# Linear attention and a token/channel mixer: releasing three weight loads by another landing, and moving one eviction in VectorE's order

## The chip, the core and the metric

The kernel runs on one core of one Trainium2 chip. The metric is the time of one execution on the device, in microseconds (us); the medians below are over runs of the same kernel.

The engines are called as the profile calls them: PE (TensorE: matmul), PEld (its weight loads), DVE (VectorE), ACT (ScalarE), POOL (GpSimd), SP (SyncE). SP and POOL issue most of the DMA transfers here: those of SP are in the profile's queue q1, those of POOL in q0.

## The reference

There are 8 batch elements ("images"), 8 heads, 576 positions and a head dimension of 64, all float32. Linear attention comes first, then a mixer over tokens and over channels:

```python
phi = lambda x: np.where(x > 0, x, np.exp(x) - 1.0) + 1.0        # elu + 1
q_p, k_p = phi(q), phi(k)
kv  = einsum('bhsd,bhse->bhde', k_p, v);  z = k_p.sum(axis=2)
x   = einsum('bhsd,bhde->bhse', q_p, kv) / (einsum('bhsd,bhd->bhs', q_p, z)[..., None] + 1e-6)
x   = x.transpose(0, 2, 1, 3).reshape(8, 576, 512)
u   = x + (relu(x.transpose(0, 2, 1) @ w_tok1) @ w_tok2).transpose(0, 2, 1)   # 576 -> 256 -> 576
out = u + relu(u @ w_ch1) @ w_ch2                                            # 512 -> 1536 -> 512
```

## The kernel before

The eight images are worked on one after another, but overlapped: while PE does the channel products of image n, the other engines load and prepare image n+1. Nothing is reordered by a scheduler. Every step has a short name (a token) in a table, and a long string, `ORDER`, lists the tokens; the kernel calls them in that order (`for name in ORDER.split(): tok[name]()`). Each engine runs its own instructions in the order in which this list issues them, and waits on semaphores where data or buffers are not ready. An instruction that waits holds up all that stands behind it on the same engine.

The tokens that matter here, the first digit being the image:

- `1Lk0 1Lk1 1Lv1 1Lq0 1Lq1 1Lv0` (line 228): SP's loads of image 1, in this order; each brings one half (piece 0 or 1, four heads, 576 KB) of k, v or q into `k_raw`, `v_raw`, `q_raw`. The first waits for a piece of the first channel weight. `2Lq0` is the first load of image 2; it waits for piece 1 of the second channel weight `wc2` (the table `GATE`).
- `1qx0`, `1qa0`, `1qb0` (lines 252, 256, 262): elu + 1 of q's piece 0 in three steps. `x` is the exponential on ACT into `e`; `a` is max(q + 1, 1) on DVE into `y`; `b` is their minimum on DVE into `qp`. There is one `y` buffer only. `1qx1 1qa1 1qb1` are the same for piece 1, `1k..` for k.
- `1v0`, `1v1` (line 275): v's pieces to bfloat16, `1v0` on DVE and `1v1` on ACT.
- `1Q00 1Q01`, then `1Q10 1Q11` (line 320): transposes of `qp` on PE, nine for each piece; `1Qc0.` and `1Qc1.` (line 326) copy them out of PSUM, on ACT for piece 0 and on DVE for piece 1. `1K` (line 302): k times v on PE; it reads both pieces of `kp` and of the converted v.
- `0ma.`, `0mb.` (line 686): the first channel product of image 0, twelve column blocks with two matmuls each in the `a` and the `b` half. `0r.` (lines 693 and 695): relu and eviction of a block from PSUM into `cr`, on DVE for blocks 3, 6 and 9, on ACT for the others.
- `0q0` to `0q11` (line 747): the second channel product of image 0, by blocks of its contraction. `0q0` does four matmuls: row blocks 0 and 1 with contraction blocks 0 and 1. Row block 1 is summed in PSUM bank 0, which block 9 of the first product has filled, so the second matmul of `0q0` waits until `0r9` has emptied it.
- `B0 B1 B2` (line 1126): POOL's loads of pieces 1, 2 and 3 of `wc2` (`load_wc2`). Piece i holds contraction blocks 3i to 3i + 2, and is converted to bfloat16 on the way, 384 KB as written. Piece 0 is issued early. Of the other three, only `B0` has a gate, but all are in POOL's one queue:

```python
WGATE = {1: ('in', 'q', 1, 0)}
...
live["wc2", i] = after(nc.gpsimd.dma_start(out=wc2[:, m * i:m * (i + 1), :], in_=...),
                       live[WGATE[i]] if i in WGATE else None)
```

`after` makes the DMA wait for the landing of the named transfer: here of q's piece 0 of image 1. Behind `B2` on POOL come `ws02 ws04 ws14 ...` (line 816), differences of `wc2` blocks that later products use.

Around the change the list reads `... G23 0mb9 0r5 0ma11 0mb11 1qa0 1qx0 B0 0r9 0q0 B1 0r11 1qb0 B2 1qx1 1qa1 1Q00 1Q01 0q1 1Qc01 1v0 1Qc00 0q2 1qb1 1v1 1Q10 1Q11 1K ...`.

Of the kernel before, what the change touches and what calls it, by code (L numbers as in the profile page):

```python
# [30 lines left out]

GATE = {'1k0': ('wc1', 0), '2q0': ('wc2', 1), '4q0': ('u', 2, 1), '7q0': ('u', 5, 1)}

WGATE = {1: ('in', 'q', 1, 0)}

ON_DVE = {'1v0', '2v1', '0r3', '0r6', '0r9', '1r5', '1r8'}

# [28 lines left out]
ORDER = """A2 A0 A1 A3 A4 A5 A6 A8 A9 A7 A10 A12 A13 A14 A11 A16 A17 A15 A19 A18 A21 A20 A22 A23 A24 A25 A26 A27 A28 A29  # L66
A30 A33 A31 A32 A35 A34 A36 A37 A38 1Lk0 A39 1Lk1 1Lv1 A40 1Lq0 A41 1Lq1 A42 1Lv0 A43 0ma0 At2 0ma1 At3 0ma3
0mb1 0mb0 0ma6 0r0 0mb3 0r1 1ka0 0ma7 1kx0 0ma2 0ma8 0mb6 1kb0 0mb2 0r3 0mb8 0mb7 0r6 0r8 0ma4 0r7 G21 0gt
1kx1 G22 0ma9 0gv 0ma10 0mb4 1ka1 0r2 0ma5 0r4 G11 0mb10 1kb1 0mb5 0r10 G23 0mb9 0r5 0ma11 0mb11 1qa0 1qx0 B0
0r9 0q0 B1 0r11 1qb0 B2 1qx1 1qa1 1Q00 1Q01 0q1 1Qc01 1v0 1Qc00 0q2 1qb1 1v1 1Q10 1Q11 1K 1Qc11 2Lq0 ws02  # L70
1Qc10 0q3 2Lq1 1Kc0 1Kc1 2Lv0 ws04 1n20 1n01 2Lk0 1nc20 0q4 2Lk1 1nc01 2Lv1 1n10 0q5 1nc10 1n00 0q6 1nc00 1n11
0q7 1nc11 2qx0 1n21 ws14 0q8 1nc21 1f0 2qx1 2qa0 1f1 wt2 3Lq0 G24 0q9 1fr1 2qb0 1fr0 0q10 2qa1 2v0 G12 1h01
2qb1 1h00 1hu01 2qT1 ws00 0q11 1hu00 0z1 2kx0 1h10 2qT0 ws10 0z0 1h11 1hu10 1t0 1hu11 1t1 3Lv0 ws24 1g2 1tc1
1tc0 1t2 3Lq1 1t3 1gu2 1ma9 1tc3 ws12 0z2 1ma1 1ma5 1tc2 1ma4 0z3 1mb1 2v1 0o1 1mb5 1r1 1ma7 2ka0 2kx1 1mb7
G01 3Lk0 1ma10 0o0 G03 3qx0 1mb4 2kb0 0ut 1ma2 2ka1 1r4 1mb10 wt0 3Lk1 1mb2 1r7 1ma3 3Lv1 1r2 2kb1 1mb9 1r10
1ma8 3qa0 0uc 1mb8 1r5 ws20 1r9 2K 1r8 1mb3 2Kc0 2Kc1 3qb0 1ma6 1r3 2n ws30 2nd 1mb6 T00 2o0 ws34 1r6 2n1
1ma11 Tr00 2o1 ws22 1mb11 2ne 3v0 2n0 1ma0 1mb0 3qa1 T01 4Lv0 1r0 2n2 ws32 1r11 1p10 3qx1 2f0 1w13 G02 Tr01
4Lq1 1w10 1p11 3kx1 3qb1 1p20 3ka0 3kx0 2f1 1w20 G14 2fr0 4Lk0 T02 1w23 3qT1 1w30 1p50 Tr02 3kb0 1p51 2fr1
3qT0 1c0 1w40 1p21 4qx1 2g1 3ka1 1c2 1eZ 1p60 3v1 G13 1p61 2gu1 2g0 1c1 3kb1 2uT1 1p31 2gu0 4kx0 1p30 3K 4qa1
2uT0 1p71 3Kc1 1eY 3Kc0 4v0 1p70 4qb1 4Lv1 4Lq0 3n 1hY 1eW 4Lk1 U00 3ne 5Lv0 3nd 1hZ U01 3n2 U02 3o0 1hW 3n1  # L80
1p40 3n0 2x01 2x11 2s1 3o1 1p41 V0 2y11 2x02 2y01 2s2 1eX 2x15 2x21 2s3 1o 2x12 2y21 2x16 2y12 2x06 2y16 2s4
2x05 2y06 2y02 2x17 2y15 4qa0 2x26 4qx0 2x25 2y17 2x07 G04 3f0 2y25 4qb0 2y05 4ka0 2y26 4qT1 2x14 2x03 2y07
2y14 2x13 3fr0 4qT0 3f1 2y13 4kb0 2x27 5Lq0 3fr1 2y03 2x23 5Lk0 2x04 2y27 2x22 2y04 4ka1 2x24 4kx1 2y22 3gt
3g1 2y23 2y24 2w10 2p20 2w12 2p10 2w20 3gu1 2p50 2p11 2w22 3uT1 2p51 3gt1 2c0 3g0 4v1 4kb1 2w30 2p60 2p61 3gu0
2p21 2c1 3gt0 3uT0 4K 2eZ 2p70 4Kc1 2c2 2w40 3ut 2p71 4Kc0 4n 2eW 5Lq1 2p30 4nd 2hW 5Lk1 4ne 2p31 5Lv1 4n0
2p41 2hZ 4o0 4n1 2p40 3x11 3s1 3x21 4o1 3y11 3s2 3x01 4n2 5kx0 3x16 3x12 2eY 3y21 T12 3s3 5v0 2eX 2hY 3x15
3y12 3x05 3y16 3x02 5ka0 2o 3y01 3x26 3y02 6Lk0 3x25 3x06 5kb0 3y25 W0 3x22 3y26 5ka1 3x23 3y06 3x17 3y22 3y15
3x27 3s4 3y05 3x07 3y17 5kx1 T11 3y27 3x03 3y07 Tr12 6Lk1 3x14 Tr11 3y03 3x24 5kb1 3x13 3y24 4f0 3y13 5qx0
5qa0 4f1 3y14 3y23 4fr0 5qb0 3x04 4fr1 T10 3w12 3y04 5qa1 4g0 Tr10 3w10 5v1 4g1 4gu0 5qx1 3p20 4gu1 4uT0 5K
6kx1 3p21 3w20 4uT1 5qb1 3p10 5Kc1 6kx0 3w22 3p11 5qT1 3eZ 3p50 3c0 6ka1 3p51 5Kc0 5qT0 3w40 U10 3c2 3w30 U11  # L90
6Lq0 6Lq1 6kb1 U12 4s1 6ka0 3p31 V1 3p30 7Lk0 4s2 6Lv1 3p61 3eY 6Lv0 3p60 6kb0 7Lk1 5n 3c1 5nd 3hY 3p71 5ne
3p70 5n0 3hZ 4x02 5o0 3eW 4x01 4x21 5n2 4y01 3hW 3p40 4y21 4y02 4x06 6qx0 5n1 4x05 4x26 4y06 6qa1 3p41 4y05
5o1 4x11 4s3 4x03 3eX 4y11 4x25 4y26 4s4 3o 4x07 4y03 6qx1 4x12 4y07 4x16 4x27 4y25 4y12 4x04 4y16 6qb1 5f0
4y04 6qa0 6v0 4x15 4y27 4x23 4w10 4y15 4x17 6qb0 5fr0 4x22 4y17 4x13 6qT0 4x24 4y23 4x14 4y24 4y13 6qT1 5f1
4y14 4y22 6v1 7ka1 4p20 4w12 4p21 5fr1 4w20 5g1 4w22 4p10 5gu1 4p11 5g0 4w40 5uT1 4c0 4eZ 5gt 6K 5gu0 4hZ 4p50
6Kc1 6Kc0 5gt1 5uT0 7kx1 4p51 5gt0 4p60 4c2 4w30 7Lv0 6n 7kx0 7Lq0 7kb1 4p61 7Lq1 6ne 7Lv1 4p30 6nd 4c1 6n2
4p31 4p71 6n0 4p70 4eY 5x11 6o1 5x02 6o0 5y11 5s1 5x12 4eW 5x01 5s2 5x15 5y01 4hW 6n1 4p40 7v0 5x16 5y12 4p41
5y16 7ka0 5x06 5y15 5s3 5x21 5y02 7F12 5x13 5y21 4eX 4hY 5x17 5y06 5x05 5y17 5x26 5y05 7kb0 4o 5x07 5y26 5x25
5y13 5x03 5y25 5s4 5x27 7qa0 7qx0 6f0 5y07 7v1 7qb0 5x14 6f1 7qa1 7qx1 5y27 5x04 6fr0 5y03 5x22 6fr1 5x23 7qb1
5y14 5x24 5y22 5y04 7qT1 7K 5y23 5p10 7Kc1 7Kc0 5w10 7qT0 5y24 6g0 5w30 6g1 5w12 5w20 5p20 6gu1 5p50 5p11 5w22  # L100
6uT1 6gu0 5p21 5c0 5p51 5eZ 6uT0 5p60 5c2 5w40 7n 5hZ 7nd 5p61 7ne 5p31 7n1 5c1 7F15 5p30 7o1 7o0 5p70 7n2
5p71 6s1 5eY 6x21 6x01 6s2 5hY 7n0 6x11 6y01 6x12 6y11 6x06 6y21 6s3 6x15 5eW 6y06 6x16 6x02 5hW 6y16 6x05
6y02 5p40 6y12 7F14 6x26 6s4 6y15 6x17 7F11 6x25 6y26 6x07 7F10 6y05 5p41 6y25 W1 6x13 5eX 6x03 6y07 6x23 7F13
6x27 6y03 6x22 5o 6x04 6y22 7f0 6y17 6y23 7f1 7fr0 6y27 6y04 6x14 6y13 7fr1 6x24 6y14 6w30 7g0 6y24 6w10 6p10
7gu0 7g1 6w12 7uT0 6p11 6w20 6p50 6w22 6c0 5ut 6p20 7gu1 6p51 7F2 7uT1 7gt 6p61 7gt0 6p60 6w40 7x12 6c1 7gt1
6p21 6c2 7F4 7ut 6p71 6eZ 7x11 6p70 7s1 6hZ 7x02 6eW 7x01 6p30 7y01 6hW 6p31 7y11 7y02 7x05 7s2 6p40 7y12 7y05
7s3 7x06 7s4 7x16 7y06 6eY 7x03 6p41 6hY 7x15 6eX 7c1 7y15 7F3 6o 7y16 7x21 7cr1 7y03 7x13 7y21 7x17 7c5 7y17
7x07 7x26 7y07 7x22 7y26 7x25 7y22 7x14 7x27 7y14 7x04 7y25 7c4 7y04 7y27 7cr5 7x23 7w10 7cr4 7x24 7y23 7c3
7y24 7w30 7w20 7c2 7y13 7w14 7c0 7cr2 7w12 7w40 7cr3 7p50 7w34 7cr0 7w22 7p51 7w24 7w42 7p10 7w44 7ts1 7p11
7ta1 7R11 7R51 7p20 7w32 7t5 7R10 7ts2 7R50 7p61 7tb1 7p31 7R61 7ts4 7R20 7p30 7R31 7tr5 7p60 7tr1 7ts3 7p71  # L110
7R60 7p21 7t6 7R21 7R30 7p70 7R71 7D200 7tr6 7t3 7D711 7D710 7ta2 7D201 7tr3 7D210 7R70 7tb2 7p41 7D311 7tr2
7D310 7t7 7D211 7R41 7td20 7p40 7D411 7tr7 7D410 7t4 7td21 7R40 7D700 7D701 7tr4 7td70 7td71"""


@with_exitstack
def kernel(
# [1007 lines left out]
    def load_wc2(i):  # L1124
# [3 lines left out]
            in_=moe_w_ch2[128 * m * i:128 * m * (i + 1), :].rearrange("(k p) d -> p k d", p=128)),  # L1128
            live[WGATE[i]] if i in WGATE else None)

# [67 lines left out]
```

## Time and profile before

| | |
|---|---|
| median of 3 runs | 245.08 us (244.67 to 245.19) |
| profiled execution, its span from the first to the last instruction | 243.4 us; the median of the runs is 1.68 us more, the time around the span |
| granted TensorE clock, mean | 0.998 |
| PE busy | 233.1 us, 96% of the span |
| DVE, ACT, POOL busy | 211.5 us (87%), 136.4 us (56%), 81.2 us (33%) |
| DMA | 48.42 MB, mean 199 GB/s |
| SP's queue q1, POOL's queue q0 | 51.3% and 25.5% of 16 engines |
| chain that ended last | PE 84%, DMA 9%, POOL 3% |

The profile is of one execution. A row of its timeline gives start, length, engine, source line, operation, output and inputs, and in brackets how long the engine was idle before the row and what ended that. A view of the waits lists who waited for whom: total, times, longest. A view of stretches gives for each its length, then the busy time of PE, PEld, DVE, ACT and POOL, the granted clock, the share of the DMA engines and GB/s. A view of the DMA queues gives for each, in a stretch of time, packets, MB, and the time that its packets took as a share of 16 engines.

### The profile page before, as it was taken

How to read it: one execution, taken by the hardware profiler on the slowest of the kernel's cores; microseconds unless marked ns; L12 is line 12 of the kernel's file. 1: busy time of each engine (PE TensorE's matmuls, PEld its weight loads, DVE VectorE, ACT ScalarE, POOL GpSimd, SP SyncE). 2: the span in 40 equal slices, each digit the busy share in tenths (PEclk: the TensorE clock that was granted, in tenths of full speed). 3: DMA queues.
4: the chain of work that ended last, by engine and by line, in shares of the span. 5: the costliest groups of instructions: out<-in, count | busy, mean ns of one | idle time of the engine just before them, and what ended most of it. 6: DMA issues, size and time to landing. Idle time of an engine off the chain costs nothing.

```text
span 243.4 us, 6361 instructions
## 1 busy us (share of the span) xinstructions
PE 233.1 (96%) x2597; PEld 174.2 (72%) x2616; DVE 211.5 (87%) x387; ACT 136.4 (56%) x224; POOL 81.2 (33%) x88
## 2 busy tenths in 40 slices
PE   7889989999999999999999999999999999999991
PEld 3575445464677686789867887688778867888881
DVE  5955786999999989999999999999999599867661
ACT  4773782669788277327994297448923542347000
POOL 8870044076910620035200520206015810440730
PEclk9999999999999999999999999999999999999999
DMA  6999989999979989978948989495782285143035
GB/s 230 278 202 260 317 260 234 409 283 286 365 225 198 270 265 161 247 97 305 285 127 175 370 262 200 82 260 178 161 138 40 44 171 112 24 91 81 3 80 180
DMA packets 49805, 48.42 MB, mean 199 GB/s; under 512 B 30064, under 2 KB 35568, under 8 KB 49776
## 3 DMA queue, kind: packets, MB, share of 16 engines
q1 hardware_dynamic: 41664, 35.00, 51.3%
q0 software_dynamic: 7472, 12.22, 25.5%
q10 hardware_dynamic: 640, 0.79, 1.0%
q8 instruction: 20, 0.33, 0.6%
q14 instruction: 9, 0.07, 0.1%
HBM read 35.85 MB, written 9.44 MB: 186 GB/s over the span
## 4 chain that ended last, share of the span: by engine, by line
PE 84%; DMA 9%; POOL 3%; issue 1%; DVE 1%; SPq 1%; POOLq 0%; DVEq 0%
PE ps L970 27%; PE ps L928 23%; PE ps L747 6%; PE ps L448 6%; DMA q_raw<-in_q_dram 5%; PE ps L459 4%; PE ps L686 4%; DMA wc<-in_moe_w_ch_dram 4%; PE ps L711 2%; PE ps L733 2%; PE ps L302 2%; PE ps L1024 2%; PE ps L387 2%; POOL qT L1111 1%; POOL cr L233 1%
## 5 line engine op out<-in xcount | busy, mean ns | idle before, releaser
L970 PE MATMUL ps<-k_raw,v_raw 128*128 128x256 bf16 x252 | 31.8, 273 | 0.0
L943 ACT COPY v_raw<-ps 128x512 f32<-128x512 f32 x30 | 17.0, 595 | 22.7 <-PE ps L928 21.5
L970 PEld LDWEIGHTS <-cr 128*128 128x128 bf16 x252 | 24.4, 98 | 4.8
L970 PEld LDWEIGHTS <-v_raw 128*128 128x128 bf16 x252 | 24.1, 98 | 3.8 <-issue 0.4
L928 PEld LDWEIGHTS <-swc 128*128 128x128 bf16 x240 | 23.4, 98 | 3.1
L681 DVE CUSTOM_DVE_ANT_0 cr<-ps,v_raw 128x512 bf16<-128x512 f32 x30 | 20.1, 684 | 4.5 <-PE ps L928 2.5
L928 PEld LDWEIGHTS <-wc 128*128 128x128 bf16 x216 | 21.1, 98 | 3.6
L928 PE MATMUL ps<-crt,swc 128*128 128x256 bf16 x180 | 23.1, 273 | 0.0
L252 ACT ACTIVATE e<-q_raw 128x1152 bf16<-128x1152 f32 x16 | 18.7, 1167 | 6.7 <-DMA q_raw<-in_q_dram 6.7
L686 PE MATMUL ps<-uT,wc 128*128 128x512 bf16 x91 | 21.6, 379 | 0.4 <-issue 0.2
L970 PE MATMUL ps<-wc,cr 128*128 128x256 bf16 x168 | 21.6, 273 | 0.0
L1071 POOL TENSOR_TENSOR obuf<-obuf,w 128x512 f32<-128x512 f32 x6 | 8.2, 1360 | 38.6 <-ACT w L1058 19.5
L252 ACT ACTIVATE e<-k_raw 128x1152 bf16<-128x1152 f32 x16 | 18.5, 1166 | 3.2 <-DMA k_raw<-in_k_dram 2.6
L1071 POOL TENSOR_TENSOR obuf<-obuf,q_raw 128x512 f32<-128x512 f32 x6 | 8.2, 1374 | 35.6 <-DVE obuf L1064 35.6
L928 PE MATMUL ps<-uT,wc 128*128 128x256 bf16 x144 | 19.5, 273 | 0.0
L1064 DVE TENSOR_TENSOR obuf<-ps,u 128x512 f32<-128x512 f32 x24 | 16.4, 685 | 2.5 <-PE ps L970 2.4
L1071 POOL TENSOR_TENSOR obuf<-obuf,part 128x512 f32<-128x512 f32 x6 | 7.7, 1289 | 26.5 <-DVE dens L400 18.5
L413 DVE TENSOR_TENSOR x<-ps,dens 128x768 bf16<-128x768 f32 x18 | 16.6, 930 | 0.0
L686 PEld LDWEIGHTS <-wc 128*128 128x128 bf16 x96 | 8.9, 98 | 10.0 <-issue 0.6
L470 DVE TENSOR_TENSOR u<-ps,x 128x1024 bf16<-128x1024 f32 x12 | 14.6, 1220 | 0.1
L836 DVE TENSOR_TENSOR v_raw<-cr 128x512 bf16<-128x512 bf16 (+3 forms) x24 | 14.5, 620 | 0.0
L448 PE MATMUL ps<-x,w 128*128 128x512 bf16 x50 | 13.9, 379 | 0.3
(168 smaller groups left out, 514.3 us busy)
## 6 DMA issues: line engine op xcount, KB each, us to landing
k_raw<-in_k_dram SPq DMA_DIRECT2D x16, 576.0 KB, 6.8
q_raw<-in_q_dram SPq DMA_DIRECT2D x16, 576.0 KB, 6.3
v_raw<-in_v_dram SPq DMA_DIRECT2D x14, 576.0 KB, 7.6
out_dram<-obuf POOLq DMA_DIRECT2D x12, 512.0 KB, 6.0
wc<-in_moe_w_ch_dram POOLq DMA_DIRECT2D x8, 384.0 KB, 9.3
out_dram<-obuf POOLq DMA_DIRECT2D x4, 256.0 KB, 7.3
cr<-in_v_dram POOLq DMA_DIRECT2D x2, 288.0 KB, 7.6
out_dram<-obuf POOLq DMA_DIRECT2D x4, 128.0 KB, 4.8
```

The costliest lines, as they stand in the source:

```text
L252: nc.scalar.activation(out=ebuf[EBUF[f"{n}{nm}{c}"]], in_=f, func=AF.Exp)
L413: nc.vector.tensor_tensor(out=xv[:, :, rc0:rc0 + 3], in0=nd_tile(n, m)[:, :, k0:k0 + 6, 0:D].rearrange("p i (q a) d -> p i q a d", a=2), i ...
L448: nc.tensor.matmul(out=banks(f"{n}f")[:, mt], lhsT=w1t[:, b, ms] if r == R else w1[:, r, ms], rhs=x[b][:, r, :], start=(r == 0), stop=(r = ...
L470: nc.vector.tensor_tensor(out=u[b][:, rs], in0=banks(f"{n}g{i}"), in1=x[b][:, rs], op=ALU.add)
L681: nc.vector._custom_dve(TENSOR_ADD_SAT, out=o, in0=ps, in1=c, s0=3.4028234663852886e38, s1=0.0)
L686: nc.tensor.matmul(out=bank(f"{n}m{mc}"), lhsT=wc1[:, kj, 128 * mc:128 * mc + 128], rhs=uTj[b][:, kj] if n < 2 - U1 else uT[b][:, :, kj], ...
L747: nc.tensor.matmul(out=bank(f"U{p}{t}"), lhsT=crt[:, kc, :] if t == 8 else cr[b][:, kc, 128 * r:128 * r + 128], rhs=wc2[:, kc, :], start=( ...
L928: nc.tensor.matmul(out=ps[:, j], lhsT=lhs[:, k_, 128 * j:128 * (j + 1)], rhs=rhs[:, :, k_], start=(first and j == 0 and k_ == 0), stop=(k_ ...
L943: nc.scalar.copy(out={1: c1, 6: c6, 5: c5}[i], in_=ps)
L970: nc.tensor.matmul(out=ps, lhsT=lhs[:, k_], rhs=rhs[:, k_], start=(first and not skip and k_ == 0), stop=(k_ == KH - 1), skip_group_check= ...
L1064: nc.vector.tensor_tensor(out=slots(f"{n}P", 4)[:, d::2, HC[c]], in0=pair_tile(n, "X" if z == "W" else z), in1=u[n % 2][:, d::2, HC[c]], o ...
L1071: nc.gpsimd.tensor_tensor(out=o, in0=o, in1=part[i], op=ALU.add)
```

## The change

`B0`, and with it `B1` and `B2` behind it, waits for the landing of v's piece 1 of image 1 instead of q's piece 0. SP issues that v load just before that q load. And `0r9`, the eviction of block 9 of image 0, stands ahead of `1qa0` on DVE, where it stood behind it. The orders of PE, ACT, POOL and SP stay the same.

```diff
-WGATE = {1: ('in', 'q', 1, 0)}
+WGATE = {1: ('in', 'v', 1, 1)}
...
-... 0mb9 0r5 0ma11 0mb11 1qa0 1qx0 B0 0r9 0q0 B1 0r11 1qb0 B2 1qx1 1qa1 ...
+... 0mb9 0r5 0ma11 0mb11 0r9 1qa0 1qx0 B0 0q0 B1 0r11 1qb0 B2 1qx1 1qa1 ...
```

The rest of `ORDER` is the same tokens in the same order, broken into lines elsewhere.

More of the change, by code (lines that the diff above doesn't have):

```diff
@@ L68 @@
 0mb1 0mb0 0ma6 0r0 0mb3 0r1 1ka0 0ma7 1kx0 0ma2 0ma8 0mb6 1kb0 0mb2 0r3 0mb8 0mb7 0r6 0r8 0ma4 0r7 G21 0gt
[L69 to L112, printed above, removed]
+1kx1 G22 0ma9 0gv 0ma10 0mb4 1ka1 0r2 0ma5 0r4 G11 0mb10 1kb1 0mb5 0r10 G23 0mb9 0r5 0ma11 0mb11 0r9 1qa0 1qx0
@@ new lines @@
+B0 0q0 B1 0r11 1qb0 B2 1qx1 1qa1 1Q00 1Q01 0q1 1Qc01 1v0 1Qc00 0q2 1qb1 1v1 1Q10 1Q11 1K 1Qc11 2Lq0 ws02 1Qc10
+0q3 2Lq1 1Kc0 1Kc1 2Lv0 ws04 1n20 1n01 2Lk0 1nc20 0q4 2Lk1 1nc01 2Lv1 1n10 0q5 1nc10 1n00 0q6 1nc00 1n11 0q7
+1nc11 2qx0 1n21 ws14 0q8 1nc21 1f0 2qx1 2qa0 1f1 wt2 3Lq0 G24 0q9 1fr1 2qb0 1fr0 0q10 2qa1 2v0 G12 1h01 2qb1
+1h00 1hu01 2qT1 ws00 0q11 1hu00 0z1 2kx0 1h10 2qT0 ws10 0z0 1h11 1hu10 1t0 1hu11 1t1 3Lv0 ws24 1g2 1tc1 1tc0
+1t2 3Lq1 1t3 1gu2 1ma9 1tc3 ws12 0z2 1ma1 1ma5 1tc2 1ma4 0z3 1mb1 2v1 0o1 1mb5 1r1 1ma7 2ka0 2kx1 1mb7 G01
@@ new lines @@
+3Lk0 1ma10 0o0 G03 3qx0 1mb4 2kb0 0ut 1ma2 2ka1 1r4 1mb10 wt0 3Lk1 1mb2 1r7 1ma3 3Lv1 1r2 2kb1 1mb9 1r10 1ma8
+3qa0 0uc 1mb8 1r5 ws20 1r9 2K 1r8 1mb3 2Kc0 2Kc1 3qb0 1ma6 1r3 2n ws30 2nd 1mb6 T00 2o0 ws34 1r6 2n1 1ma11
+Tr00 2o1 ws22 1mb11 2ne 3v0 2n0 1ma0 1mb0 3qa1 T01 4Lv0 1r0 2n2 ws32 1r11 1p10 3qx1 2f0 1w13 G02 Tr01 4Lq1
+1w10 1p11 3kx1 3qb1 1p20 3ka0 3kx0 2f1 1w20 G14 2fr0 4Lk0 T02 1w23 3qT1 1w30 1p50 Tr02 3kb0 1p51 2fr1 3qT0 1c0
+1w40 1p21 4qx1 2g1 3ka1 1c2 1eZ 1p60 3v1 G13 1p61 2gu1 2g0 1c1 3kb1 2uT1 1p31 2gu0 4kx0 1p30 3K 4qa1 2uT0 1p71
@@ new lines @@
+3Kc1 1eY 3Kc0 4v0 1p70 4qb1 4Lv1 4Lq0 3n 1hY 1eW 4Lk1 U00 3ne 5Lv0 3nd 1hZ U01 3n2 U02 3o0 1hW 3n1 1p40 3n0
+2x01 2x11 2s1 3o1 1p41 V0 2y11 2x02 2y01 2s2 1eX 2x15 2x21 2s3 1o 2x12 2y21 2x16 2y12 2x06 2y16 2s4 2x05 2y06
+2y02 2x17 2y15 4qa0 2x26 4qx0 2x25 2y17 2x07 G04 3f0 2y25 4qb0 2y05 4ka0 2y26 4qT1 2x14 2x03 2y07 2y14 2x13
+3fr0 4qT0 3f1 2y13 4kb0 2x27 5Lq0 3fr1 2y03 2x23 5Lk0 2x04 2y27 2x22 2y04 4ka1 2x24 4kx1 2y22 3gt 3g1 2y23
+2y24 2w10 2p20 2w12 2p10 2w20 3gu1 2p50 2p11 2w22 3uT1 2p51 3gt1 2c0 3g0 4v1 4kb1 2w30 2p60 2p61 3gu0 2p21 2c1
@@ new lines @@
+3gt0 3uT0 4K 2eZ 2p70 4Kc1 2c2 2w40 3ut 2p71 4Kc0 4n 2eW 5Lq1 2p30 4nd 2hW 5Lk1 4ne 2p31 5Lv1 4n0 2p41 2hZ 4o0
+4n1 2p40 3x11 3s1 3x21 4o1 3y11 3s2 3x01 4n2 5kx0 3x16 3x12 2eY 3y21 T12 3s3 5v0 2eX 2hY 3x15 3y12 3x05 3y16
+3x02 5ka0 2o 3y01 3x26 3y02 6Lk0 3x25 3x06 5kb0 3y25 W0 3x22 3y26 5ka1 3x23 3y06 3x17 3y22 3y15 3x27 3s4 3y05
+3x07 3y17 5kx1 T11 3y27 3x03 3y07 Tr12 6Lk1 3x14 Tr11 3y03 3x24 5kb1 3x13 3y24 4f0 3y13 5qx0 5qa0 4f1 3y14
+3y23 4fr0 5qb0 3x04 4fr1 T10 3w12 3y04 5qa1 4g0 Tr10 3w10 5v1 4g1 4gu0 5qx1 3p20 4gu1 4uT0 5K 6kx1 3p21 3w20
@@ new lines @@
+4uT1 5qb1 3p10 5Kc1 6kx0 3w22 3p11 5qT1 3eZ 3p50 3c0 6ka1 3p51 5Kc0 5qT0 3w40 U10 3c2 3w30 U11 6Lq0 6Lq1 6kb1
+U12 4s1 6ka0 3p31 V1 3p30 7Lk0 4s2 6Lv1 3p61 3eY 6Lv0 3p60 6kb0 7Lk1 5n 3c1 5nd 3hY 3p71 5ne 3p70 5n0 3hZ 4x02
+5o0 3eW 4x01 4x21 5n2 4y01 3hW 3p40 4y21 4y02 4x06 6qx0 5n1 4x05 4x26 4y06 6qa1 3p41 4y05 5o1 4x11 4s3 4x03
+3eX 4y11 4x25 4y26 4s4 3o 4x07 4y03 6qx1 4x12 4y07 4x16 4x27 4y25 4y12 4x04 4y16 6qb1 5f0 4y04 6qa0 6v0 4x15
+4y27 4x23 4w10 4y15 4x17 6qb0 5fr0 4x22 4y17 4x13 6qT0 4x24 4y23 4x14 4y24 4y13 6qT1 5f1 4y14 4y22 6v1 7ka1
@@ new lines @@
+4p20 4w12 4p21 5fr1 4w20 5g1 4w22 4p10 5gu1 4p11 5g0 4w40 5uT1 4c0 4eZ 5gt 6K 5gu0 4hZ 4p50 6Kc1 6Kc0 5gt1
+5uT0 7kx1 4p51 5gt0 4p60 4c2 4w30 7Lv0 6n 7kx0 7Lq0 7kb1 4p61 7Lq1 6ne 7Lv1 4p30 6nd 4c1 6n2 4p31 4p71 6n0
+4p70 4eY 5x11 6o1 5x02 6o0 5y11 5s1 5x12 4eW 5x01 5s2 5x15 5y01 4hW 6n1 4p40 7v0 5x16 5y12 4p41 5y16 7ka0 5x06
+5y15 5s3 5x21 5y02 7F12 5x13 5y21 4eX 4hY 5x17 5y06 5x05 5y17 5x26 5y05 7kb0 4o 5x07 5y26 5x25 5y13 5x03 5y25
+5s4 5x27 7qa0 7qx0 6f0 5y07 7v1 7qb0 5x14 6f1 7qa1 7qx1 5y27 5x04 6fr0 5y03 5x22 6fr1 5x23 7qb1 5y14 5x24 5y22
@@ new lines @@
+5y04 7qT1 7K 5y23 5p10 7Kc1 7Kc0 5w10 7qT0 5y24 6g0 5w30 6g1 5w12 5w20 5p20 6gu1 5p50 5p11 5w22 6uT1 6gu0 5p21
+5c0 5p51 5eZ 6uT0 5p60 5c2 5w40 7n 5hZ 7nd 5p61 7ne 5p31 7n1 5c1 7F15 5p30 7o1 7o0 5p70 7n2 5p71 6s1 5eY 6x21
+6x01 6s2 5hY 7n0 6x11 6y01 6x12 6y11 6x06 6y21 6s3 6x15 5eW 6y06 6x16 6x02 5hW 6y16 6x05 6y02 5p40 6y12 7F14
+6x26 6s4 6y15 6x17 7F11 6x25 6y26 6x07 7F10 6y05 5p41 6y25 W1 6x13 5eX 6x03 6y07 6x23 7F13 6x27 6y03 6x22 5o
+6x04 6y22 7f0 6y17 6y23 7f1 7fr0 6y27 6y04 6x14 6y13 7fr1 6x24 6y14 6w30 7g0 6y24 6w10 6p10 7gu0 7g1 6w12 7uT0
@@ new lines @@
+6p11 6w20 6p50 6w22 6c0 5ut 6p20 7gu1 6p51 7F2 7uT1 7gt 6p61 7gt0 6p60 6w40 7x12 6c1 7gt1 6p21 6c2 7F4 7ut
+6p71 6eZ 7x11 6p70 7s1 6hZ 7x02 6eW 7x01 6p30 7y01 6hW 6p31 7y11 7y02 7x05 7s2 6p40 7y12 7y05 7s3 7x06 7s4
+7x16 7y06 6eY 7x03 6p41 6hY 7x15 6eX 7c1 7y15 7F3 6o 7y16 7x21 7cr1 7y03 7x13 7y21 7x17 7c5 7y17 7x07 7x26
+7y07 7x22 7y26 7x25 7y22 7x14 7x27 7y14 7x04 7y25 7c4 7y04 7y27 7cr5 7x23 7w10 7cr4 7x24 7y23 7c3 7y24 7w30
+7w20 7c2 7y13 7w14 7c0 7cr2 7w12 7w40 7cr3 7p50 7w34 7cr0 7w22 7p51 7w24 7w42 7p10 7w44 7ts1 7p11 7ta1 7R11
@@ L115 @@
+7R51 7p20 7w32 7t5 7R10 7ts2 7R50 7p61 7tb1 7p31 7R61 7ts4 7R20 7p30 7R31 7tr5 7p60 7tr1 7ts3 7p71 7R60 7p21
+7t6 7R21 7R30 7p70 7R71 7D200 7tr6 7t3 7D711 7D710 7ta2 7D201 7tr3 7D210 7R70 7tb2 7p41 7D311 7tr2 7D310 7t7
+7D211 7R41 7td20 7p40 7D411 7tr7 7D410 7t4 7td21 7R40 7D700 7D701 7tr4 7td70 7td71"""
 @with_exitstack
```

## The prediction

> **What bounds the kernel now.** I read the waits of TensorE (PE) first, then its busy time by stretch, then the instructions around the change, engine by engine, and last what the DMA queues moved there.
>
> From 34 to 226 us nothing on PE waits for long: it is busy for 186.90 of 188.00 us between 38 and 226. A step moves the end only if it moves PE before 38, or makes PE wait later. Apart from the start, the longest wait of PE is that of its first mm4 product (L747) for a VectorE (DVE) eviction. Waits of PE, then busy time by stretch (first figures: length, PE busy):
>
> ```profile
> PE ps L747 <- DVE cr L693: 0.8, 1, 0.8
> ```
>
> ```profile
> 32.00:38.00 6.00, 5.11 (x101) 2.78 (x104) 4.83 (x8) 4.95 (x7) 2.49 (x4) 1.00 0.93 205
> 38.00:226.00 188.00, 186.90 (x2149) 144.01 (x2151) 176.21 (x315) 112.10 (x180) 56.72 (x56) 1.00 0.77 197
> ```
>
> The timeline of that place, one engine after another (start, length, operation). DVE: the six rows are `1qa0`, `0r9`, `1qb0`, `1qa1`, `1v0`, `1qb1`:
>
> ```profile
> 32.37 0.76 DVE L256 TENSOR_SCALAR y<-q_raw 128x1152 bf16<-128x1152 f32 x1 [0.91 <-DMA q_raw<-in_q_dram]
> 33.04 0.68 DVE L693 TENSOR_SCALAR cr<-ps 128x512 bf16<-128x512 f32 x1
> 33.64 0.75 DVE L262 TENSOR_TENSOR qp<-e,y 128x1152 bf16<-128x1152 bf16 x1
> 34.43 1.01 DVE L256 TENSOR_SCALAR y<-q_raw 128x1152 bf16<-128x1152 f32 x1
> 35.36 0.75 DVE L275 CAST vs<-v_raw 128x1152 bf16<-128x1152 f32 x1
> 36.02 0.75 DVE L262 TENSOR_TENSOR qp<-e,y 128x1152 bf16<-128x1152 bf16 x1
> ```
>
> PE (first product of `0q0`, its other three, `1Q00`/`1Q01`, `1Q10`/`1Q11`, `1K`), ScalarE (ACT: `1qx0`, the `1Qc0` copies, `1v1`) and GpSimd (POOL: `B0` to `B2`):
>
> ```profile
> 32.56 0.38 PE L747 MATMUL ps<-wc,cr 128*128 128x512 bf16 x1
> 33.78 0.81 PE L747 MATMUL ps<-wc,cr 128*128 128x512 bf16 x3 [0.84 <-DVE cr L693]
> 34.45 0.68 PE L320 MATMUL ps<-identity,qp 128*128 128x128 bf16 x9
> 36.83 0.68 PE L320 MATMUL ps<-identity,qp 128*128 128x128 bf16 x9
> 37.43 0.78 PE L302 MATMUL ps<-vs,kp 64*64 64x65 bf16 x72
> ```
>
> ```profile
> 32.01 1.17 ACT L252 ACTIVATE e<-q_raw 128x1152 bf16<-128x1152 f32 x1
> 35.16 1.18 ACT L326 COPY qT<-ps 128x512 bf16<-128x512 bf16 x2 [0.45 <-PE ps L320]
> 36.23 1.17 ACT L275 CAST vs<-v_raw 128x1152 bf16<-128x1152 f32 x1
> ```
>
> ```profile
> 32.40 2.47 POOL L1126 DMA_DIRECT2D wc<-in_moe_w_ch_dram  x3 [14.34 <-DMA q_raw<-in_q_dram]
> ```
>
> So PE waits for `0r9`, which stands behind `1qa0`, which waits for q. Products of 512 columns follow each other at 0.216 us (eight in the chain's piece of 1.73), so the second would have come at 32.78: 1.00 us is lost. The DMA view of single issues gives the landings (issue plus time to landing): v's piece 1 at 18.25 + 12.2 = 30.45, q's pieces at 18.76 + 13.1 = 31.86 and 19.27 + 14.0 = 33.27, v's piece 0 at 19.87 + 14.9 = 34.77, the released weight piece at 32.40 + 5.3 = 37.70.
>
> **The order on DVE.** The moved eviction costs what it did, 0.68. It can start when `0mb9` ends. The run of L686 products before `0q0` ends at 32.73; four products of 0.216 come after `0mb9`, so that is 31.87. Then `0r9` goes from about 31.92 to 32.60, inside the 0.91 us in which DVE idles today. `0q0`'s second product may start at 32.66, sooner than its 32.78: the 1.00 us is gone there, and `0q0` issues its four by 33.43.
>
> Next on PE is `1Q00`, which needs `1qb0`. `1qa0` follows `0r9`; rows follow each other 0.08 us early (32.37 + 0.76 against 33.04), so it runs from 32.52 to 33.28. `1qb0` reads it at once; such a pair near the start (6.82 + 0.83, then 7.75) shows 0.10 between them: 33.38 to 34.13. The ACT side, 32.01 + 1.17 = 33.18, is not last. PE followed `1qb0` by 0.06 (34.39, then 34.45), so `1Q00` starts at 34.19: **0.26 earlier** than 34.45. Most of the stall has only moved, to a wait for `1qb0`. With `1qa0` free, the bound is 33.18 + 0.06 + 0.75 + 0.06 = 34.05, a gain of **0.40**. That is the ceiling.
>
> Behind it, the `1Qc0` copies on ACT start at 34.90 instead of 35.16, `1v1` ends at 37.14, and `1K`, which reads it, starts at 37.17 against 37.43: 0.26 is kept. On DVE `1qa1` would run from about 34.06 to 34.82, `1v0` from 34.74 and `1qb1` from 35.40 to 36.15, before PE's own 36.42 for `1Q10`, provided that v's piece 0 has landed by 34.7. `1K` stands 0.60 behind `1Q10` (36.83, 37.43), so up to `1v0` at 35.10 costs nothing; `1v0` at 35.36, today's, uses the gain up, and each us beyond is a us lost.
>
> **The release.** `B0` waits for v's piece 1, 31.86 − 30.45 = 1.41 us sooner; by today's 0.54 from landing to issue it starts at 30.99. `B1` and `B2` are queued behind it on POOL, and so are the weight sums (first at 37.98); SP's `2Lq0` waits for the first weight piece. By themselves all come up to 1.4 us earlier, worth nothing: `0q3`, the first product that reads that piece, runs at 38.14, after 37.70 already, and PE has no stall behind it that an earlier q of image 2 would end. `0q3` moving to 37.9 keeps that cover even where the piece lands only as now. The cost is what three pieces of 384 KB do to q's piece 1 and v's piece 0, still under way until 33.27 and 34.77. Three stretches of the DMA view bear on this: 4.8 to 7.7 (POOL issues outstanding), 7.8 to 9.6, and 21 to 24 us.
>
> ```profile
> q1 hardware_dynamic: 522, 1.13, 103.3%
> ```
>
> ```profile
> q0 software_dynamic: 192, 0.22, 72.1%
> q1 hardware_dynamic: 135, 0.28, 42.9%
> ```
>
> ```profile
> q1 hardware_dynamic: 312, 0.68, 65.9%
> q0 software_dynamic: 313, 0.23, 49.4%
> ```
>
> In the first, SP's loads (q1) hold all 16 engines and POOL's queue (q0) moves no packet, though its issues began at 3.74; from 57 to 58.5, after issues from 55.45 on, it is the same. POOL's pieces came in as the loads thinned out, in the second stretch. The third is the other side: with POOL's queue already running, each moves as many packets (312, 313), and loads fall to 0.68 MB in 3 us, 227 GB/s, from 407 between 31 and 32.4. In the place of the change the loads are the ones in full flow, as in the first. So I take v's piece 0 to be late by 0 to 0.4 us only, landing at 34.8 to 35.2: 0.26 is kept in whole or in part. **Sum**, with 0.06 for that tail: −0.2 us on the profiled 243.4; with the 1.68 us between this span and the median of 245.08, 244.9 us. The bounds of this case are −0.40 and 0.
>
> The Trainium skill (DMA: Bandwidth & Descriptors, "Queues, rings and completion order") says that each DMA engine takes turns between the queues that have work, packet by packet. By that rule the pieces share the engines from their start on, which is the first rival. The 21 to 24 us stretch agrees with it (312 to 313), the 4.8 to 7.7 one does not.
>
> **Rivals.** *v's piece 0 comes late (slower).* POOL's packets first show 1.6 us or more after the issue today (none from 32.4 to 34, 51 from 34 to 35), so they could start at 32.6 and be in full flow near 33.6. A piece of loads takes 1.43 us alone and 1.43 × 407 / 227 = 2.6 shared. Sharing from 33.3 on lands v's piece 0 at 35.9, from 34.3 on at about 35.5. `1v0` then starts at 35.55 to 35.95; `1qb1`, `1Q10` and `1K` follow, and since 35.36 was today's start PE loses 0.2 to 0.6, and 0.8 if the start also takes the 0.5 that DVE needed after q's landing (31.86, 32.37). It decides from a landing of about 35.3. For it: the third stretch. Against: the first. Time: 245.6.
>
> *POOL's issues hold up `1qa0` (no change).* `1qa1` took 1.01 today, beside POOL's third issue, where such rows take 0.76. If the earlier issues (30.99 to 33.46) lengthen `1qa0` by that 0.25, the 0.26 is gone: 245.1. Against: `1qa0` today ran beside the first of them in 0.76.
>
> *More is won.* Past the ceiling of 0.40, something must come out of the 1.10 us that PE idles between 38 and 226, through loads of image 2 that land 1 us sooner: 244.5. Against: no PE wait there is named that a load ends.
>
> *The change does nothing.* It would need the v landing to come as late as q's; 1.41 us stand between them. No chance of its own.
>
> **How the numbers follow.** A measurement of this kernel tells about 0.2%, 0.49 us, from no change. Forecast 0.48, of which 0.08 beyond 0.49 faster, since runs scatter by 0.5 (244.67 to 245.19). Late v 0.33, three quarters of it slower by over 0.49. POOL on `1qa0` 0.04. More won 0.10. A late wait that I have not seen 0.05, slower. Faster 0.08 + 0.10 = 0.18; within 0.40 + 0.08 + 0.04 = 0.52; slower 0.25 + 0.05 = 0.30. Range: 244.4 (ceiling, and what more could be won) to 245.9 (the late v's upper end, 0.8). The forecast's own is 244.7 to 245.1.
>
> **What would show it.** Right: `0r9` at 31.9; no gap inside `0q0`; a new PE wait for `qp` of about 0.75 us before `1Q00`, at 34.2; POOL's issue near 31.0; `1v0` before 35.2; `1K` at 37.2. Wrong: `1v0` with an idle time ended by the v load, `1Q10` after 36.9, `1qa0` at 1.0 us, or a PE wait after 38 that is not there today.

## The result and the profile after

The changed kernel takes 244.65 us (median of 14 runs, 243.91 to 245.37) against 245.32 (14 runs of the kernel before, 244.67 to 246.11): ratio 0.9964, 95% interval 0.9949 to 0.9978. Two later comparisons of the same pair gave 0.997 (0.9954 to 0.9985) and 0.9974 (0.9957 to 0.999). It is faster by about 0.3%, 0.6 to 0.9 us, where 0.2 us was forecast. One execution of the kernel before, in a later comparison, ran at a granted clock of 0.757 and took 306.11 us; no ratio counts it. The profiled execution of the changed kernel took 244.9 us, its span is 243.1.

That profile is 0.35 us ahead of the one before from the start of the first channel product on (its first matmul at 20.48 against 20.83), before any instruction that the change touches; so times are compared below from that matmul, from the start of `0q0`, or from the landing of q's piece 0. The waits of PE:

```profile
PE ps L320 <- DVE qp L262: 2.2, 2, 1.4
```

The wait for `cr` is gone from the list. A wait for `qp` has taken its place (two of them; the other 1.4 us, near 8, is from the start of the kernel). Busy time by stretch, columns as before:

```profile
32.00:38.00 6.00, 5.10 (x105) 2.93 (x105) 5.01 (x8) 5.01 (x7) 2.32 (x3) 1.00 1.12 231
38.00:226.00 188.00, 186.89 (x2124) 144.09 (x2140) 176.11 (x315) 111.96 (x180) 55.88 (x56) 1.00 0.73 196
```

Behind 38 us PE is as full as before. The DMA share from 32 to 38 rose from 0.93 to 1.12: more of the weight pieces now lies there. The timeline of DVE (`0r9`, `1qa0`, `1qb0`, `1qa1`, `1v0`, `1qb1`), PE (`0q0`, `1Q00`, `1Q10`, `1K`), ACT and POOL:

```profile
31.54 0.69 DVE L693 TENSOR_SCALAR cr<-ps 128x512 bf16<-128x512 f32 x1 [0.23 <-PE ps L686]
32.25 1.03 DVE L256 TENSOR_SCALAR y<-q_raw 128x1152 bf16<-128x1152 f32 x1
33.44 0.76 DVE L262 TENSOR_TENSOR qp<-e,y 128x1152 bf16<-128x1152 bf16 x1 [0.16 <-ACT e L252]
34.23 0.76 DVE L256 TENSOR_SCALAR y<-q_raw 128x1152 bf16<-128x1152 f32 x1
34.99 0.77 DVE L275 CAST vs<-v_raw 128x1152 bf16<-128x1152 f32 x1
35.67 0.75 DVE L262 TENSOR_TENSOR qp<-e,y 128x1152 bf16<-128x1152 bf16 x1
```

```profile
32.38 1.03 PE L747 MATMUL ps<-wc,cr 128*128 128x512 bf16 x4
34.25 0.68 PE L320 MATMUL ps<-identity,qp 128*128 128x128 bf16 x9 [0.85 <-DVE qp L262]
36.49 0.67 PE L320 MATMUL ps<-identity,qp 128*128 128x128 bf16 x9
37.09 0.78 PE L302 MATMUL ps<-vs,kp 64*64 64x65 bf16 x72
```

```profile
32.24 1.16 ACT L252 ACTIVATE e<-q_raw 128x1152 bf16<-128x1152 f32 x1 [0.29 <-DMA q_raw<-in_q_dram]
36.03 1.17 ACT L275 CAST vs<-v_raw 128x1152 bf16<-128x1152 f32 x1
```

```profile
31.19 2.33 POOL L1126 DMA_DIRECT2D wc<-in_moe_w_ch_dram  x3 [13.39 <-DMA v_raw<-in_v_dram]
```

`0q0` now runs in one piece, and the stall stands before `1Q00`. `1K` comes 4.71 us behind the start of `0q0` (37.09, 32.38), where it took 4.87 (37.43, 32.56). This execution was not a good one: q's piece 0 landed at 32.16 (31.86 before). `1qa0` also took 1.03 instead of 0.76, but that cost nothing here: `1qb0` waited 0.16 us more for the exponential on ACT, which q's landing had held up. The queues from 31.5 to 32.5 us, while POOL is already issuing its pieces (from 31.19 on):

```profile
q1 hardware_dynamic: 190, 0.41, 104.7%
```

POOL's queue (q0) has no line in that stretch. That alone does not show that the loads keep it out: its first packet came at 32.83, 1.64 us after the issue, and in an experiment below (release by v's piece 0), where the engines were idle at the issue, it still came 1.47 us after. v's piece 0 landed at 34.97, against 34.73 before (the prediction's 34.77 adds a time to landing that is given to a tenth).

### The profile page after: what moved, and what is told of

Its sections match the earlier page's. It is cut to its first block, busy times and chain, and to the rows that moved or that the text cites. A ratio compares the mean times of both kernels' runs of the same rounds, so it can differ in the third digit from the quotient of the medians.

```text
span 243.1 us, 6362 instructions
## 1 busy us (share of the span) xinstructions
PE 232.1 (95%) x2597; PEld 173.9 (72%) x2616; DVE 211.6 (87%) x387; ACT 136.4 (56%) x224; POOL 80.6 (33%) x88
## 4 chain that ended last, share of the span: by engine, by line
PE 83%; DMA 9%; POOL 3%; issue 1%; SPq 1%; DVE 0%; ACT 0%; POOLq 0%; ACTq 0%
PE ps L970 27%; PE ps L928 23%; PE ps L747 6%; PE ps L448 6%; DMA q_raw<-in_q_dram 5%; PE ps L459 4%; PE ps L686 4%; DMA wc<-in_moe_w_ch_dram 4%; PE ps L711 2%; PE ps L733 2%; PE ps L302 2%; PE ps L1024 2%; PE ps L387 2%; POOL qT L1111 1%; PE ps L523 1%; PE ps L478 1%
## 5 line engine op out<-in xcount | busy, mean ns | idle before, releaser
L256 DVE TENSOR_SCALAR y<-k_raw 128x1152 bf16<-128x1152 f32 x16 | 12.0, 753 | 3.0 <-DMA k_raw<-in_k_dram 2.8
```

## The experiments

Each was timed beside 23 to 35 executions of the kernel before. There are 12 executions of each version, but eight of the third comparison of both edits and four with the release by v's piece 0. A ratio is the time over that of the kernel before, with its 95% interval.

**The eviction alone (two runs).**

```diff
-WGATE = {1: ('in', 'v', 1, 1)}
+WGATE = {1: ('in', 'q', 1, 0)}      # on the changed kernel
```

> The eviction moved ahead of the elu alone; the release stays at q's piece 0. Theory A (the order on VectorE is the whole gain: after q's landing, 1Q00 follows through the exponential in 2.09 us, 34.25 less 32.16, where before it took 2.59, 34.45 less 31.86): ratio 0.996 to 0.998, as with both edits, and in its profile no gap inside 0q0 and 1Q00 2.0 to 2.2 us behind q's landing. Theory B (the release is the gain, through weights and later loads that land sooner; the stall only changes its name): ratio 0.999 to 1.001. Theory C (each brings a part, or only both together): 0.998 to 0.999.

Measured: 0.9999 (0.9978 to 1.0021). Its profile, waits of PE between 33 and 41 and PE's timeline, with `0q0`, `1Q00` and, last, `0q3`:

```profile
PE ps L747 <- DMA wc<-in_moe_w_ch_dram: 1.4, 2, 1.1
```

```profile
33.11 1.02 PE L747 MATMUL ps<-wc,cr 128*128 128x512 bf16 x4 [0.26 <-DMA wc<-in_moe_w_ch_dram]
34.68 0.68 PE L320 MATMUL ps<-identity,qp 128*128 128x128 bf16 x9 [0.55 <-DVE qp L262]
...
39.62 1.02 PE L747 MATMUL ps<-wc,cr 128*128 128x512 bf16 x3 [1.13 <-DMA wc<-in_moe_w_ch_dram]
```

`0r9` does its part, `1Q00` follows q's landing (32.59) by 2.09 us, and yet nothing is gained: `0q3` waits for weight piece 1, which landed at 39.58. Of the 16 engines that bring a piece, 14 had finished theirs by 37.99; two were 1.6 us behind. (The other wait of the list, 0.26 before `0q0`, is for piece 0 of `wc2`, which the change does not touch; it landed at 33.07.) This is the slowest of the 12 executions, 246.46 us against a median of 245.55. So I formed theory D, that the release is worth the cover in front of `0q3` (the time by which piece 1 lands ahead of it), and ran the kernel again.

> The moved eviction alone, q's release, once more: its first profile showed PE waiting 1.30 us before 0q3 for weight piece 1, which landed at 39.58 there and at 37.72 in the profile of before. Theory D (the release is worth the end of that wait, since the landing scatters by 2 us from one execution to the next, and the 0.4 us of cover that it had in the profile of before is not there in others): ratio 0.998 to 1.001, piece 1 landing between 37.5 and 39.6, and PE waiting before 0q3 by whatever that landing is past 1K's end, about 37.8. Theory A (the eviction is the whole gain, the first profile of this kernel an accident): ratio 0.996 to 0.998 and no wait before 0q3.

Measured: 0.9993 (0.9976 to 1.0011). This time piece 1 landed at 37.65 and `0q3` ran unhindered at 37.83. So the wait comes in some executions only. The ratio stays at no change both times, and theory A (the order is the whole gain) falls.

**The release alone (two runs).**

```diff
-WGATE = {1: ('in', 'q', 1, 0)}
+WGATE = {1: ('in', 'v', 1, 1)}      # on the kernel before
```

> The release by v's piece 1 alone; the eviction stays behind the elu. Theory A: ratio 0.999 to 1.002, with the 1.0 us gap inside 0q0 as before, and the weight piece about 1 us sooner for nothing. Theory B: ratio 0.996 to 0.998. Theory C: 0.998 to 0.999.

Measured: 0.9994 (0.9972 to 1.0016). Piece 1 landed at 36.98, sooner than before, and the gap inside `0q0` stayed:

```profile
33.72 0.81 PE L747 MATMUL ps<-wc,cr 128*128 128x512 bf16 x3 [0.93 <-DVE cr L693]
```

> The release by v's piece 1 alone, again. With the release worth 0.3 to 0.6 us by its cover and the gap inside 0q0 still there: ratio 0.9975 to 0.9995; 1K 4.8 to 5.1 us behind the start of 0q0. Theory A: 0.999 to 1.002.

Measured: 0.9993 (0.9981 to 1.0006), `1K` 4.57 us behind the start of `0q0` (37.43, 32.86; below the 4.8 to 5.1 expected, since `0q0` itself began late). So neither edit alone moves the time by what these comparisons can tell, and theory B (the release is the gain) falls too. Theory C is left, but which half of it is open: the four ratios of single edits would add up to 0.1% where both edits bring 0.3%, which speaks for a gain that needs both, yet each interval has room for a part of 0.1% by itself.

**Both edits again (two runs).** No edit.

> Both edits once more, for a second profile beside the same runs of before. All theories: ratio 0.995 to 0.998. Theory A adds: 1Q00 about 2.1 us behind q's landing whatever that is; and where q lands by 31.9 on this profile's clock, 1Q00 at 34.0 to 34.2. Theory B adds: 1Q00 no earlier against the start of 0q0 than in the profile of before, and the gain in a later stretch.

Measured: 0.997 (0.9954 to 0.9985). In this execution `1qa0` took 0.75 and q's piece 0 landed at 31.67:

```profile
32.23 0.75 DVE L256 TENSOR_SCALAR y<-q_raw 128x1152 bf16<-128x1152 f32 x1
...
36.74 0.78 PE L302 MATMUL ps<-vs,kp 64*64 64x65 bf16 x72
```

`0q0` began at 32.29, so `1K` stood 4.45 us behind it.

> Both edits, beside the two splits: ratio 0.995 to 0.998; piece 1 landing near 36.5 to 37.0, 1K 4.4 to 4.7 us behind the start of 0q0 (4.71 and 4.45 in the first two), no PE wait before 0q3.

Measured: 0.9974 (0.9957 to 0.999), piece 1 at 36.59, `1K` 4.52 us behind (36.77, 32.25), no wait before `0q3`.

**The kernel before again.**

> The kernel before, unchanged, for a second profile of it and for the scatter of such a comparison. All theories: ratio 0.998 to 1.002. Theory A adds: 1Q00 2.5 to 2.7 us behind q's landing; the gap inside 0q0 grows or shrinks with that landing.

Measured: 0.9996 (0.998 to 1.0012), which shows how far such a comparison strays by itself. The second profile of the kernel before is of one further execution:

> The kernel before, unchanged, for one more profile. Theory D: piece 1 lands between 37.5 and 39.6; where past the end of 1K (38.1 in the first profile), PE waits for it before 0q3. Theory A: no such wait; the gap inside 0q0 near 1.0 us.

One time of 245.03 us. PE's gap before the three products of `0q0`, and DVE's `1qa1`:

```profile
33.62 0.81 PE L747 MATMUL ps<-wc,cr 128*128 128x512 bf16 x3 [1.06 <-DVE cr L693]
```

```profile
34.27 1.01 DVE L256 TENSOR_SCALAR y<-q_raw 128x1152 bf16<-128x1152 f32 x1
```

Piece 1 landed at 37.33, `0q3` ran at 37.98: no wait. `1Q00` stood 2.59 us behind q's landing (34.29, 31.70), the same as in the first profile.

**The release moved further, on the changed kernel.**

```diff
-WGATE = {1: ('in', 'v', 1, 1)}
+WGATE = {1: ('in', 'k', 1, 1)}      # by k's piece 1; then by v's piece 0: ('in', 'v', 1, 0)
```

> Both edits, but the release by k's piece 1 of image 1 (landing at 28.8 in the profile with both edits), some 1.9 us sooner than v's. Turn by turn (the queues share the engines packet by packet): q's piece 0 lands 0.5 us or more later, v's piece 0 at 35.5 or later, 1Q00 later by as much, ratio against before 0.998 to 1.002, slower than with both edits. Loads first (POOL's pieces get in only as the loads thin out): loads land as with both edits, piece 1 no more than 0.5 us sooner, ratio 0.995 to 0.998.

Measured: 1.0024 (1.0006 to 1.0042), slower than before. q's piece 0 landed as ever (31.71), piece 1 at 36.56: no sooner than by v's release (36.45 to 36.94), though its issue began 1.4 to 1.9 us sooner (29.30). Here POOL's pieces did stand behind the loads: from 30.5 to 32.3 us, 1.2 to 3.0 us after the issue, SP's queue alone moved packets.

```profile
q1 hardware_dynamic: 337, 0.74, 104.2%
```

But v's piece 0, the last load, was late, at 35.12, and DVE waited for it with `1qb1` behind:

```profile
35.14 0.77 DVE L275 CAST vs<-v_raw 128x1152 bf16<-128x1152 f32 x1 [0.50 <-DMA v_raw<-in_v_dram]
```

```profile
36.62 0.68 PE L320 MATMUL ps<-identity,qp 128*128 128x128 bf16 x9 [0.32 <-DVE qp L262]
```

This looks like the slower rival of the prediction, at an earlier release, but it is not shown. With the release by v's piece 0 (next), where POOL issues nothing before 35.75, that load landed at 35.21 all the same; and this profile is of the fastest of the 12 executions (245.06 us, median 246.01), so what slowed the others is not in it.

> Both edits, but the release by v's piece 0 of image 1 (landing about 34.7), some 4 us later than by piece 1. Theory D: B0 starts near 35.3, piece 1 lands 4.5 to 6 us behind that, at 39.8 to 41.2, and PE waits 2.0 to 3.4 us before 0q3, which shows as such in time: ratio against before 1.005 to 1.011. Theory A: the release does not matter, ratio 0.996 to 0.998.

Measured: 1.0106 (1.006 to 1.0152). Piece 1 landed at 40.68 and PE waited for it:

```profile
40.72 0.59 PE L747 MATMUL ps<-wc,cr 128*128 128x512 bf16 x2 [2.62 <-DMA wc<-in_moe_w_ch_dram]
```

So the release does set `0q3` when it is late enough. With the eviction moved, the best of the four releases tried is the one that the change takes.

**Is it the cover in front of `0q3`?** Piece 1 in two loads, block 3 ahead:

```diff
+        cuts = [m * i, m * i + 1, m * (i + 1)] if i == 1 else [m * i, m * (i + 1)]
+        for k0, k1 in zip(cuts, cuts[1:]):
             live["wc2", i] = after(nc.gpsimd.dma_start(out=wc2[:, k0:k1, :], ...
```

> The moved eviction, q's release, and weight piece 1 in two loads: contraction block 3 alone (128 KB), then blocks 4 and 5. Block 3, which is all that 0q3 reads, should land some 1 us sooner than the whole piece does under q's release (36.4 to 36.8 against 37.3 to 37.7), without any earlier release. Theory D (the release by v is worth the cover in front of 0q3): ratio 0.996 to 0.998, as with both edits, and no PE wait before 0q3. If the release works in another way (loads of image 2, POOL's sums): 0.999 to 1.001, as with the eviction alone.

Measured: 0.9997 (0.9984 to 1.001). Block 3 landed at 35.64, 2.3 us ahead of `0q3` at 37.94, and still nothing was gained. Theory D had forecast the whole gain here, and that did not come. But the split brings a loss of its own, so it does not settle what the cover is worth. POOL issued its four loads from 32.51 to 35.34, beside `1qa1` and `1v0`, which took 1.07 and 0.89, and `1Q10` came 2.57 us behind `1Q00` (36.62, 34.05) instead of 2.24 as with both edits, 0.33 us later:

```profile
34.02 1.07 DVE L256 TENSOR_SCALAR y<-q_raw 128x1152 bf16<-128x1152 f32 x1
35.02 0.89 DVE L275 CAST vs<-v_raw 128x1152 bf16<-128x1152 f32 x1
```

> Both edits and the same split. Theory D: the cover in front of 0q3 was 0.9 to 1.0 us in the two profiles with both edits and seldom too short, so 0 to 0.3 us more at most: ratio 0.995 to 0.998. If block 3 takes engines from q and v at 32 to 34 us: 0.998 to 1.000.

Measured: 0.9975 (0.9963 to 0.9987), the same as both edits without the split in the same runs (0.9974); `1K` 4.32 us behind the start of `0q0` (36.69, 32.37). With the split, too, the earlier release is worth 0.2% (0.9975 against 0.9997). No version beat the changed kernel.

## Why the prediction was right, and where its size was off

**What moves the end.** Right. From `1f0`, the first matmul of image 1's token mixing (44.64 us before), to the start of the last matmul, PE took 193.6 to 193.8 us in each of the 13 profiles used, of six versions besides the two kernels. So nearly all differences come about ahead of it. There, much of the scatter is q's piece 0, which landed 10.96 to 11.68 us after the first channel product began, whatever the order and the release. Counted from that landing, the executions of a version agree better (us):

| | `1Q00` starts | piece 1 lands | `0q3` starts |
|---|---|---|---|
| before | 2.59, 2.59 | 5.86, 5.63 | 6.28, 6.28 |
| the eviction alone | 2.09, 2.09 | 6.99, 5.48 | 7.03, 5.66 |
| the release alone | 2.58, 2.59 | 5.17, 5.16 | 6.13, 6.13 |
| both edits | 2.09, 2.24, 2.09 | 4.78, 4.78, 4.79 | 5.64, 5.78, 5.68 |

**The order on DVE.** Right in its steps. The prediction had `1Q00` 1.63 us behind the start of `0q0` (34.19, 32.56); the later two profiles with both edits have 1.62 (33.91, 32.29) and 1.64 (33.89, 32.25). In the first, where q landed later, it was 1.87. That most of the stall only moves, to a wait for `qp`, is in every one.

**The first mis-sized term: what is kept behind `1Q00`.** I let `1v1` on ACT set `1K` and so held the gain to 0.26. The profile before had `1v1` end at 37.40 and `1K` start at 37.43, which I read as a wait. It was a coincidence: in the second profile with both edits `1K` starts at 36.74, and `1v1` ends only at 36.85 (35.68 + 1.17). By the code, the first half of `1K` reads only what `1v0` has written. `1K` follows the transposes, so the 0.14 us that `1Q10` waited before came back as well. Measured from the start of `0q0`, `1K` stood at 4.87 and 5.09 before and at 4.71, 4.45 and 4.52 with both edits: 0.42 us less in the mean, where I had taken 0.2 and called 0.40 the ceiling.

**The second: the release, priced at nothing.** That was the step that failed. The forecast put the whole gain on the order, which alone brings 0.01% and 0.07% by its two ratios; with the release added, in the same comparison as the first of these, it is 0.3%. The prediction took `0q3` to be covered (by 0.44 us, and still after it had moved to 37.9) from the one profile that it had. The table shows how thin that was. Under q's release piece 1 and `0q3` both count from q's landing. The moved eviction brings `0q3` from 6.28 to 5.66 behind it, and piece 1 landed 5.48 to 6.99 behind it, so two of those four landings (5.86 and 6.99) come too late for the earlier `0q3`. Under v's release it landed 4.78 to 5.17 behind q, ahead of `0q3` in all five. That is the likely reason why the eviction's gain shows only with the release; it rests on four landings, and the split, which was to test it, has a loss of its own, so it stays open how much of the 0.3% this is.

**POOL beside DVE.** A second loss is ended by either edit. In both profiles before, `1qa1` took 1.01, and `1Q10` came 0.14 us late for it. What decides is when the row starts. POOL's third issue took 34.11 to 34.86 in the first profile before, and `1qa1` began 0.32 us into it, at 34.43. With the eviction alone both begin almost together:

```profile
34.20 1.04 POOL L1126 DMA_DIRECT2D wc<-in_moe_w_ch_dram  x1
34.24 0.76 DVE L256 TENSOR_SCALAR y<-q_raw 128x1152 bf16<-128x1152 f32 x1
```

Over all profiles, the four rows of `1qa0` or `1qa1` that began 0.26 to 0.32 us into an issue took 1.01 to 1.07; the eight that began within 0.05 us of an issue's start took 0.75 or 0.76, and that issue 0.96 to 1.04 instead of 0.75; two that began in the last 0.1 us of an issue took 0.76. With the release by v, `1qa1` took 0.76 in all six profiles, since POOL is done issuing by then or within 0.1 us of it. I had used the 0.76 in the sum without seeing what it hung on. The Trainium skill (SBUF — State Buffer, "SBUF: two separate sides") says that VectorE in some of its modes and GpSimd hold one port pair in turn, whoever comes first, and that the other blocks. These rows look like it, though a row that began 0.04 us after the issue was not held up; that this lock lengthened them was not tested.

From q's landing on, both edits put `0q3` 0.58 us ahead (5.70 against 6.28 in the mean); the three ratios give 0.6 to 0.9 us. What is missing may lie in executions of the kernel before in which piece 1 is late: the two that were profiled, of 245.08 and 245.03 us, are faster than its medians of 245.3 to 245.5. No profile shows one.

**The rivals.** *v's piece 0 late*: not at this release, with landings of 34.97, 34.52 and 34.66 with both edits against 34.73 and 34.38 before; by k's piece 1 `1v0` waited 0.50 us for it, from a cause that is not shown. The stretches with no POOL packet under full loads were the right ones to go by here; the turn-by-turn rule would have had v's piece 0 at 35.5 to 35.9. *POOL holds up `1qa0`*: it did so in one of three profiles with both edits (1.03), which is the execution shown above, and cost nothing there. *More is won*: yes, but not where I put it; PE idles no less between 38 and 226.

The forecast's own range, −0.40 to 0, ends short of the measured 0.6 to 0.9 us; the wide range held it. That is luck in part: its lower end was set by a rival whose mechanism, loads of image 2, did not bring the gain, and the kernel before measured 245.32 beside the change, not the 245.08 that the forecast counts from. "Within 0.2%" had a chance of 0.52 and "faster" 0.18. The first was too high for a reason: it rested on a cover of 0.44 us and on landings of one execution, which scatter by more than that.

## What to carry to other kernels

A stall that one profile shows could be priced here from its rows to 0.02 us in two of three executions, but a cover of less than a microsecond under a DMA landing could not: take the landings of several executions before calling a wait hidden. Count times from the event on which both sides of a wait hang, here q's landing; the scatter that they share then drops out. Two edits that each show no gain can show one together, where one wait stands right behind the other; so undo each alone before crediting either. When a GpSimd queue issues DMAs, look at what VectorE does during the issuing, not only at when the data lands.

## What the runs showed of the hardware

A piece of 384 KB is brought by 16 engines, and the slowest sets its landing: with the eviction alone, 14 of them had finished at 37.99 us in one execution, the last at 39.58.

A new POOL transfer can be kept waiting while SP's loads fill the engines. Issued at 29.30 by k's piece 1, it got no packet from 30.5 to 32.3 us against 337 of SP's; on idle engines (release by v's piece 0) the first came 1.47 us after the issue. So an issue 1.4 to 1.9 us sooner brought piece 1 no sooner (36.56 against 36.45 to 36.94).

A VectorE row of 0.76 us took 1.01 to 1.07 when it began 0.26 to 0.32 us into a DMA issue of POOL; begun within 0.05 us of the issue's start it kept its 0.76, and the issue took 0.96 to 1.04 instead of 0.75.
